# The first values of a fused attention and ELU kernel: from GpSimd's DMA queue to SyncE's, and into the buffer that first holds keys

## The chip, the cores and the metric

The kernel runs on one core of a Trainium2 chip. The metric is the device time of one execution in microseconds. Before the change it is 358.51 us, the median of three runs (358.48 to 359.07).

Engines are named as in the profile: PE (TensorE), DVE (VectorE), ACT (ScalarE), POOL (GpSimd) and SP (SyncE). PEld is PE's loading of weights. A q behind a name (SPq, POOLq) means an instruction that starts a DMA from that engine's instruction stream. Each engine takes its instructions strictly in the order written into its own stream; between engines they wait on semaphores.

## The reference

Eight batches with eight heads, 576 rows in each and a head size of 64, in float32:

```
proj = x @ w_phi                                   # 64 -> 128, for q and for k
proj = proj - max(abs(proj), axis=-1)
phi  = [exp(proj), exp(-proj)]                     # 256 features
kv   = phi(k)^T @ v ;  z = sum of phi(k) over the rows
out  = (phi(q) @ kv) / (phi(q) . z + 1e-6)         # linear attention
x    = out laid side by side over the heads        # 4608 x 512
h    = x @ w_in ;  g = elu(h) ;  y = g @ w_out     # 512 -> 2048 -> 512
```

The result is y, 4608 x 512 in float32.

## The kernel before, in words

**Tiling.** A batch is worked on in two "quads" of four heads each. Of the 576 rows of a head, 512 are the main part (four rows to each of 128 partitions) and 64 are the tail. A quad transposes its keys and queries on PE (L628), projects them (L689 keys and queries for the maxima, L864 queries again with features in the partitions), takes the maxima on DVE (L710), the exponentials on ACT (L757 keys, L944 queries), and the factors em that carry the maxima of the keys (L786, ACT). POOL multiplies the values by these factors: `scales` (L800), four products of the main part for a quad (`v_scaled`, L808, two for each half of the heads) and two of the tails (`v_tail_scaled`, L818). PE then sums keys times values (L992), and queries times that (L1060 and L1074). DVE combines and inverts (L1095, L1101, L1155), POOL makes x (L1172 in batch 0), and PE transposes x (L1259). From then on x @ w_in (L1354 for the first chunk, L1339 after), ELU and g @ w_out (L1443) run beside the attention of later batches.

**Order of the work.** A planner (`Planner.run`, L169) goes through the operations in simulated time and takes, on every engine, the free one of lowest rank; the ranks stand in a string (RANKS). Its result is the order in which instructions are written, and with it the order of every engine's stream. It also writes "fill" matmuls of zeros (L1651) where it expects PE to idle in the first 60 us. Semaphores follow from the tiles that an instruction reads and writes.

**Buffers.** `staged(b, n)` (L417) gives the tile for keys (n = 0), queries (1), values (2) and tails (3) of batch b, two buffers for each kind in turn. The values' buffers are float32, and the profile names both v_b. In the first stage a values' buffer is used for something else as well: the first four heads of keys of batch 0 are loaded into it as float32, two heads by ACT's queue and two by SP's (L1517), and ACT turns them into bf16 (`cast`, L1550). The tile is called k_first, and it is the buffer of the values of batch 1.

**Loads of the first batch.** `load_first` (L1578) writes them into POOL's stream, in the order of ranks: tails of k, heads 4 to 7 of k, heads 0 to 3 of v, heads 0 to 3 and 4 to 7 of q, heads 4 to 7 of v, tails of q. Then come keys and values of batch 1, and weights. A load of v of one half is 512 KB in float32. The tails of v go through SP's queue in eight DMAs (L456), the first four held back by a copy on DVE (`hold_tails`, L1637) until a maximum of the keys is there. v of batches 2 and later goes through SP's queue as well (L427).

**POOL's DMA semaphores.** POOL's DMAs take turns on eight semaphores, so the ninth DMA in its stream waits for the first to have landed, the tenth for the second, and so on. These waits stand in POOL's stream in front of the instruction, and everything behind waits with it.

Of the kernel before, what the change touches and what calls it, by code (L numbers as in the profile page):

```python
# [326 lines left out]
def kernel(  # L327
# [10 lines left out]
    nc = tc.nc  # L338
# [78 lines left out]
    def staged(b, n):  # L417
        if (b, n) not in kqv:
            kqv[b, n] = stage.tile(
                [P, 2 * H * D if n == 3 else BW],  # L420
                FP32 if n == 2 else BF16,
                name="kqvt"[n] + "_b",
            )
        return kqv[b, n]

    def load_main(eng, n, b, h0, h1):
        eng.dma_start(  # L427
            out=staged(b, n)[:, h0 * HW:h1 * HW].rearrange("p (h n) -> p h n", n=HW),
            in_=(k, q, v)[n][b, h0:h1, 0:MAIN, :].rearrange(
                "h (p t) d -> p h (t d)", t=NT  # L430
            ),
        )
# [34 lines left out]
    def load(name, mb, cost, fn, deps=()):  # L467

        key = -6.0 + 0.001 * len(landed)
        landed[name] = add(  # L470
            {"POOL": cost}, fn, deps or [landed["begun"]], key=key, load=mb,
            alone=3.0 + mb / plan.MB_PER_US_OF_ONE,
        )
# [1034 lines left out]
        tc.manual_schedule(engines={E.PE, E.DVE, E.Activation, E.Pool, E.SP})  # L1508
    )
    wst = moesm.tile([P, CHUNK], FP32, name="e_sb")[:, 0:F]  # L1510
    staged(0, 2)
    k_first = staged(1, 2)
    for c, eng in enumerate((nc.scalar, nc.sync)):
        w = wst[c * D:(c + 1) * D, :]
        if c:
# [56 lines left out]
    def load_kq_tails(n, b):  # L1572
        if n < 2:
            load((b, n, 1), 0.15, 0.7, lambda e: load_tails(nc.gpsimd, n, b))
        else:
            load_v((b, n, 1), 0.5, 2.6, lambda e: load_tails(nc.sync, n, b), [])

    def load_first(n, part):  # L1578
        if part == 1:
            load_kq_tails(n, 0)  # L1580
            return
        h = 2 * part
        load(
            (0, n, part), 0.57 if n == 2 else 0.54, 0.8,
            lambda e: load_main(nc.gpsimd, n, 0, h, h + 4),
        )

    for n, part in ((0, 1), (0, 2), (1, 0), (1, 1), (2, 0), (2, 1), (1, 2), (2, 2)):
        load_first(n, part)
# [98 lines left out]
```

## Time and profile before

| | |
|---|---|
| median of three runs | 358.51 us |
| the profiled execution's own time | 358.15 us |
| its span in the profile | 356.40 us |
| PE busy | 344.2 us (97%) |
| DVE, ACT, POOL busy | 264.4, 261.6, 243.5 us |
| clock granted to PE | 0.999 |
| DMA moved | 43.46 MB, mean 122 GB/s |

The profile gives times from the start of the span. A page of it shows totals over 356 us; the stage that the change touches is the first 45 us, and it is read from the timeline of single instructions, from the answers on who waited for whom, and from the DMA queues in short windows. In the DMA view, q0 (software_dynamic) is POOL's queue and q1 (hardware_dynamic) is SP's; q10 is ACT's. Behind each name stand packets, MB, and the time of the packets as a share of the 16 DMA engines, which goes over 100% where packets overlap. Sizes of a DMA are those of its destination. The fill matmuls count as busy PE, so a busy PE in the first 40 us isn't a PE with work.

### The profile page before, as it was taken

What the parts mean: (1) busy time and instruction counts of PE and PEld (TensorE: products, weight loads), DVE (VectorE), ACT (ScalarE), POOL (GpSimd) and SP (SyncE); (2) the same over time, 40 slices, a digit from 0 to 9 for tenths busy, and PEclk for the clock granted to TensorE, in tenths of its full rate; (3) what the DMA queues carried; (4) which work ended last, traced back from release to release, by engine and by line L of the source; (5) the groups of instructions that cost most, each with busy time, mean ns of one, the idle gap of its engine ahead of it and who ended that gap; (6) DMA issues with size and microseconds to landing.
All of it is one profiled execution on the core that took longest, in us unless ns stands there. A gap on an engine that the chain in (4) does not pass through costs nothing.

```text
span 356.4 us, 9086 instructions
## 1 busy us (share of the span) xinstructions
PE 344.2 (97%) x3439; PEld 205.5 (58%) x3484; DVE 264.4 (74%) x571; ACT 261.6 (73%) x575; POOL 243.5 (68%) x342
## 2 busy tenths in 40 slices
PE   7899999999999999999999999999999999999995
PEld 6677779556654664565655565555656545454444
DVE  6999799989997899878879867985888744425300
ACT  5998988997779888788878788868677545445311
POOL 8899987979867896988736983599365844335200
PEclk9999999999999999999999999999999999999999
DMA  7999999995896896799847422622032110010023
GB/s 164 256 234 209 206 194 217 180 179 162 129 140 131 139 228 106 161 181 138 96 92 204 96 65 64 195 64 65 32 93 64 30 36 29 29 62 29 29 62 87
DMA packets 84268, 43.46 MB, mean 122 GB/s; under 512 B 54656, under 2 KB 77696, under 8 KB 84224
## 3 DMA queue, kind: packets, MB, share of 16 engines
q1 hardware_dynamic: 57632, 26.59, 32.6%
q0 software_dynamic: 25760, 15.47, 30.6%
q10 hardware_dynamic: 832, 0.82, 0.8%
q8 instruction: 27, 0.44, 0.5%
q14 instruction: 17, 0.14, 0.1%
HBM read 36.77 MB, written 9.44 MB: 130 GB/s over the span
## 4 chain that ended last, share of the span: by engine, by line
PE 85%; ACT 6%; DVE 3%; DMA 3%; issue 2%; POOL 1%; ACTq 0%; POOLq 0%
PE po L1443 32%; PE ph L1339 31%; PE pkv L992 5%; PE pk L689 4%; PE ph L1354 4%; PE pn L1046 3%; DMA t_b<-in_q_dram 3%; PE pq L864 2%; ACT Eq L944 2%; ACT EK L757 2%; DVE tot L1095 1%; PE pnt L1074 1%; DVE tot L1101 1%; ACT e_sb L1367 1%; PE pk L671 1%
## 5 line engine op out<-in xcount | busy, mean ns | idle before, releaser
L1443 PE MATMUL po<-w_out_sb,gT 128*128 128x512 bf16 (+2 forms) x584 | 133.0, 368 | 1.3 <-issue 0.2
L1371 POOL TENSOR_SCALAR u_sb<-e_sb 128x512 bf16<-128x512 f32 x144 | 88.5, 620 | 66.6 <-ACT e_sb L1367 62.8
L1383 DVE SCALAR_TENSOR_TENSOR gT<-u_sb,ph 128x512 bf16<-128x512 bf16 x144 | 96.1, 679 | 36.0 <-POOL u_sb L1371 35.7
L1367 ACT ACTIVATE e_sb<-ph 128x512 f32<-128x512 f32 x144 | 86.5, 613 | 38.2 <-PE ph L1339 31.5
L1339 PE MATMUL ph<-xT,w_in 128*128 128x512 bf16 x427 | 106.0, 380 | 1.8 <-DVE gT L1383 0.5
L1443 PEld LDWEIGHTS <-gT 128*128 128x128 bf16 x608 | 55.2, 98 | 58.3 <-issue 2.5
L1339 PEld LDWEIGHTS <-w_in 128*128 128x128 bf16 x512 | 54.5, 114 | 45.6 <-issue 3.0
L757 ACT ACTIVATE EK<-pk 128x512 bf16<-128x512 f32 x128 | 68.4, 630 | 7.5 <-PE pk L689 6.7
L944 ACT ACTIVATE Eq<-pq 128x512 bf16<-128x512 f32 x128 | 68.7, 638 | 5.6 <-PE pq L864 5.5
L808 POOL TENSOR_TENSOR vs<-v_b,em 128x512 bf16<-128x512 f32 x64 | 65.9, 1048 | 0.1
L710 DVE TENSOR_REDUCE m_q<-pk 128x4 f32<-128x512 f32 (+1 forms) x80 | 48.2, 629 | 10.5 <-PE pk L689 8.5
L710 DVE TENSOR_REDUCE m_k<-pk 128x4 f32<-128x512 f32 (+1 forms) x80 | 47.6, 626 | 4.7 <-PE pk L689 4.6
L1143 POOL TENSOR_TENSOR x<-tot,rec 128x576 bf16<-128x576 f32 x28 | 31.8, 1157 | 10.2 <-DVE rec L1139 10.0
L1471 ACT COPY o_sb<-po 128x512 f32<-128x512 f32 (+2 forms) x29 | 16.3, 561 | 30.6 <-PE po L1443 28.7
L1095 DVE TENSOR_TENSOR tot<-pn,w 128x260 f32<-128x260 f32 x64 | 26.6, 423 | 8.6 <-PE pn L1046 7.2
L1101 DVE TENSOR_TENSOR tot<-tot,pn 128x260 f32<-128x260 f32 x64 | 26.4, 419 | 0.5
L1046 PEld LDWEIGHTS <-Eq 128*128 128x128 bf16 x448 | 20.1, 97 | 9.1
L818 POOL TENSOR_TENSOR vst<-v_tail,em 128x260 bf16<-128x260 f32 x32 | 19.7, 624 | 7.2 <-ACT em L786 7.2
L1046 PE MATMUL pn<-kv,Eq 128*128 128x65 bf16 x448 | 21.9, 193 | 0.1
L992 PE MATMUL pkv<-vs,EK 128*128 128x65 bf16 x512 | 20.5, 194 | 0.0
L992 PEld LDWEIGHTS <-EK 128*128 128x128 bf16 x512 | 18.4, 98 | 2.9 <-DVE m_q L710 0.4
L1354 PE MATMUL ph<-xT,w_in 128*128 128x256 bf16 x128 | 17.6, 274 | 0.2 <-DVE xT L1266 0.2
(93 smaller groups left out, 315.3 us busy)
## 6 DMA issues: line engine op xcount, KB each, us to landing
out_dram<-o_sb SPq DMA_DIRECT2D x32, 256.0 KB, 2.4
v_b<-in_v_dram SPq DMA_DIRECT2D x6, 1024.0 KB, 5.6
k_b<-in_k_dram POOLq DMA_DIRECT2D x7, 512.0 KB, 8.0
q_b<-in_q_dram POOLq DMA_DIRECT2D x7, 512.0 KB, 8.7
w_out_sb<-in_moe_w_out_dram POOLq DMA_DIRECT2D x4, 512.0 KB, 17.5
w_in<-in_moe_w_in_dram POOLq DMA_DIRECT2D x2, 1024.0 KB, 18.8
v_b<-in_v_dram POOLq DMA_DIRECT2D x2, 512.0 KB, 8.6
v_b<-in_v_dram POOLq DMA_DIRECT2D x1, 1024.0 KB, 13.8
```

The source lines that it names most:

```text
L710: nc.vector.tensor_reduce(dst, src, axis=AX.X, op=ALU.max, apply_absolute_value=True)
L757: nc.scalar.activation(EK()[:, 2 * c + par, sg, :] if c < 2 else EKt[:, sg, :], bank.tile[:, 0:n, :].rearrange("p a b -> p (a b)"), ACT.Ex ...
L808: nc.gpsimd.tensor_tensor(st["vs"][:, sg, :, r, 0:D], kqv[b, 2][:, o:o + 2 * HW].rearrange("p (c n d) -> p c n d", c=2, d=D), by_head(st[" ...
L944: nc.scalar.activation(dst, src, ACT.Exp, scale=1.0 - 2.0 * sg)
L992: nc.tensor.matmul(pkv[:, c, sg, :], st["EK"][:, 2 * s + t % 2, sg, (2 * c + t // 2) * F:(2 * c + t // 2 + 1) * F,] if t < NT else EKt[:, ...
L1046: nc.tensor.matmul(pt[:, t, :], st["Eq"][:, par, s, sg, o:o + P], st["kv"][:, s, c, sg, :], start=True, stop=True,)
L1339: nc.tensor.matmul(ph, w_in_of(ct, jt), xTs[ch][:, ct, :] if ch < B else xT_tail[:, ct // 2, :, ct % 2, :], start=(ct == 0), stop=(ct == N ...
L1354: nc.tensor.matmul(bank.tile[:, j, :], w_in_of(ct, jt + j), xTs[ch][:, ct, hf * CHUNK // 2:(hf + 1) * CHUNK // 2], start=(j == 0 and ct == 0),
L1367: nc.scalar.activation(t["e"], flat(bank.tile), ACT.Exp)
L1371: nc.gpsimd.tensor_scalar(t["u"], t["e"], -1.0, 1.0, op0=ALU.add, op1=ALU.mult)
L1383: nc.vector.scalar_tensor_tensor(dst, u, 0.0, bank.tile, op0=ALU.min, op1=ALU.max)
L1443: nc.tensor.matmul(bank.tile, gTs[ch][:, jt, tt * P:(tt + 1) * P], w_out_sb[:, jt, o0:o1], start=(jt == 0), stop=(jt == N_JT - 1),)
```

## The change

k_first becomes the buffer of the values of batch 0, where it was that of batch 1. The two halves of v of batch 0 leave POOL's stream and go to SP's, both at the place of the second one's operation. What the planner counts for these two operations, and all ranks, stay as they are.

```diff
-    staged(0, 2)
-    k_first = staged(1, 2)
+    k_first = staged(0, 2)
+    staged(1, 2)
...
         h = 2 * part
-        load(
-            (0, n, part), 0.57 if n == 2 else 0.54, 0.8,
-            lambda e: load_main(nc.gpsimd, n, 0, h, h + 4),
-        )
+
+        def heads(e):
+            if n < 2:
+                load_main(nc.gpsimd, n, 0, h, h + 4)
+            elif part:
+                for g in (0, 4):
+                    load_main(nc.sync, n, 0, g, g + 4)
+
+        load((0, n, part), 0.57 if n == 2 else 0.54, 0.8, heads)
```

In the streams of the engines this gives the following. POOL's has two DMAs fewer, and all else in it stands in the same order. SP's has the two DMAs right behind its load of k_first, ahead of the eight tails of v; the first of them waits for both of ACT's casts, since it writes over what they read. The load of v of batch 1 on POOL, which waited for the casts before, doesn't any more. PE, DVE and ACT have the same instructions in the same order.

The waits in POOL's stream shift with the two DMAs gone. The first load of w_out waits for no DMA (before: heads 4 to 7 of k); the tails of k of batch 1 wait for the tails of k of batch 0 (before: heads 0 to 3 of v); the first load of w_in waits for heads 4 to 7 of k (before: heads 0 to 3 of q). From the second load of w_out on, each DMA waits for the same one as before.

## Prediction

> **What bounds the kernel now.** The page gives PE 97% of the span, and the waits of PE between 44 and 300 us sum to 0.7 us, so from there on PE is full and a shift of the start is a shift of the end. The start is another stage. Busy time by stretches (us, then PE, PEld, DVE, ACT, POOL) shows it:
>
> ```profile
> 10.00:15.00 5.00, 4.07 (x71) 3.21 (x68) 4.68 (x10) 5.00 (x15) 4.20 (x7) 1.00 1.33 244
> 15.00:20.00 5.00, 4.44 (x73) 3.12 (x71) 4.80 (x10) 4.90 (x15) 4.99 (x8) 1.00 1.19 304
> 20.00:25.00 5.00, 4.92 (x99) 3.55 (x98) 4.48 (x12) 5.00 (x18) 4.98 (x9) 1.00 1.16 205
> 25.00:30.00 5.00, 4.50 (x109) 3.82 (x105) 4.89 (x17) 4.89 (x14) 4.98 (x8) 1.00 1.25 205
> 30.00:35.00 5.00, 4.71 (x76) 3.85 (x74) 4.96 (x17) 3.89 (x11) 4.96 (x8) 1.00 1.18 212
> ```
>
> POOL, DVE and ACT are all nearly full, and the DMA column is over 1. So I read POOL's timeline (start, duration, what; in brackets the idle time before and its releaser):
>
> ```profile
> 6.64 0.93 POOL L427 DMA_DIRECT2D k_b<-in_k_dram  x1
> 7.51 0.95 POOL L427 DMA_DIRECT2D v_b<-in_v_dram  x1
> 9.50 0.56 POOL L404 DMA_DIRECT2D w_out_sb<-in_moe_w_out_dram  x1 [1.04 <-DMA k_b<-in_k_dram]
> 10.84 0.60 POOL L436 DMA_DIRECT2D t_b<-in_k_dram  x1 [0.78 <-DMA v_b<-in_v_dram]
> 11.44 0.34 POOL L800 CAST vs<-em 128x32 bf16<-128x32 f32 x1
> 11.62 1.05 POOL L808 TENSOR_TENSOR vs<-v_b,em 128x512 bf16<-128x512 f32 x1
> ```
>
> From 10.84 us to about 45 us POOL has no gap that is listed; the two of 1.04 and 0.78 us are its only waits between 10 and 46. PE hangs on that stream directly; PE's longest wait of 10 to 46 us, in sum, is
>
> ```profile
> PE tr L1259 <- POOL x L1172: 0.5, 2, 0.3
> ```
>
> (29.59 and 30.74 us), and the vst products that end at 20.60 stand just ahead of the first sum of keys times values at 20.85. POOL from its first L808 on is therefore the line on which a delay passes to PE. ACT and DVE are as full, so a POOL that starts earlier gains little.
>
> **The DMA side.** POOL's queue works as a FIFO. v heads 0 to 3 are issued at 3.09 and land after 7.5 us (about 10.6, which releases POOL at 10.84); queries of batch 1, issued at 15.45, land after 16.7 us, at 32.15, and PE's L628 on them starts at 32.68. On SP's queue I look at how long an issue takes to its first packets while POOL's queue is busy. The first tail of v is issued at 8.47. The windows 8.4:9 and 12.5:13 have (packets, MB, share):
>
> ```profile
> q0 software_dynamic: 145, 0.12, 112.6%
> ...
> q0 software_dynamic: 165, 0.10, 108.8%
> q1 hardware_dynamic: 52, 0.01, 19.2%
> ```
>
> From 9 to 12.4 us there is no packet of q1: 4.0 us from issue to first packet. The transpose issued at 48.74 has its first packets at 52.7, again 4.0. With POOL's queue empty, at 84.0 us, v of a later batch has its first packets after about 1.6 us, runs at 347 to 369 packets of 1 KB per us, and lands 5.4 us after its issue.
>
> **What the Trainium skill says.** "DMA: Bandwidth & Descriptors", Issuing engines are not separate DMA queues: all queues run on the same 16 engines, and another issuer saves only its own issue time. The trace agrees: q0 falls from 382 packets per us alone to 243 beside q1's 238 (53:54 us). The same page, Queues, rings and completion order: engines go round robin over the queues by packet. That is this 1:1; beside the tails of v it was less for q1 (163 to 298 at 15:16). The same page, Latency and other measured facts: about 600 ns to a hardware queue's first byte. The trace shows 1.6 us free and 4.0 us under load; I use these.
>
> **The change part by part.**
>
> *Two issues leave POOL.* 0.77 + 0.79 = 1.56 us before its first product. POOL isn't late there, it waits afterwards. With the waits of the semaphores shifted, w_out's and t_b's issues are over at about 8.1, and L800 can start when em is there: the two L786 end at 10.53. So L808 could start at about 10.9 instead of 11.62, at best 0.7 us sooner, if its values are there.
>
> *SP's two issues.* The first waits for both casts; ACT's second ends at 5.54 + 0.62 = 6.16, so the first issue is at about 6.3. Behind it in SP's stream stand the second half and the tails of v. SP's tails before are held to 8.47 by DVE, and the two issues cost some 0.6 us each (0.59 and 0.57 for the two first ones on SP), so SP is free at 7.5: the issues cost nothing on SP itself; their packets are the matter.
>
> *When do heads 0 to 3 land?* First packet: 1.6 us later if free, 4.0 under load; POOL's queue is over 100% from 5.5 us on, hence I take 4.0, so 10.3. Then 512 packets of 1 KB. Without v in front of them, q and its tails are through POOL's queue by then, and the keys of batch 1 are in it, which are cast. Cast packets alone ran at 356 to 375 per us; shared 1:1 that is about 182 for each, so 512 packets take 2.8 us (bounds 1.4 alone, 3.9 at the tails' share of 163 to 298). Landing after the last packet 0.5 us (0.7 at 84.0; 0.2 to 0.4 for k_first). Sum 6.3 + 4.0 + 2.8 + 0.5 = 13.6. L808 starts at 13.6 instead of 11.62: **+2.0 us** on POOL's stream.
>
> *What the stall delays.* Behind L808 stand w_in's first load, three more products, q of batch 1, w_in, w_out, the tails' products. All the DMAs queue behind some 10 us of backlog in a FIFO, so they don't land later by being issued 2 us later. The products do come later: vst ends at 22.6, L992 starts at 22.8, x at 30.7 becomes 32.6, and PE with it. q of batch 1, at 32.15, no longer matters. PE's gaps before 37 us, including the fill of 0.50 at 36.23, come behind the same x, so they shift too, and I take 0 as absorbed. Cover for other delays: heads 4 to 7 of v are needed at 21.28 + 2.0 and should land near 18; the tails of v behind them in SP's queue land near 21, needed at 19.38 + 2.0. This is close.
>
> *Gains.* q and its tails land 2 to 4 us sooner. PE waited 0.4 us for the tails (15.54) and 0.17 for q, but ACT is full between 10 and 20 us (9.90 of 10), so this gives at most 0.1 us, and the later POOL stall hides it. Bytes are the same, so the backlog's end stays.
>
> Sum on the profiled execution: 358.15 + 2.0 = 360.15. The median of the runs is 0.36 higher: 358.51 + 2.0 = **360.5 us**.
>
> **Rivals.**
>
> *Quick start.* If SP's packets come after 1.6 us, as at 84.0, and share 1:1, v lands at 6.3 + 1.6 + 2.8 + 0.5 = 11.2, L808 starts about 0.4 us sooner, and with v at full rate (1.4 us) em is the limit, 0.7 sooner. PE then runs into q of batch 1 at 32.15, 0.5 us ahead of its L628: so -0.4 us, at most -0.7: 357.8 to 358.1. It decides from a landing before 11.6 on. For it: POOL's backlog is only 2 us old at 6.3. Against: 4.0 us in both loaded cases. Only its end, at -0.7, could be told from no change.
>
> *Hidden.* A landing at 11.6 to 12.3 (first packet after 2.5 to 3 us) gives 0 to +0.7: 358.5 to 359.2. PE's fills and ACT's backlog at 20 to 24 us could absorb a further few tenths.
>
> *SP's queue starved.* When POOL's queue reaches v of batch 1, its packets are large: 95 per us at 18:19, 3.7 KB each. At 1:1, SP's 1 KB packets get under 100 per us: heads 4 to 7 take 4 us and more, to about 18, the 512 tail packets behind them 3 to 5 us more, to 21 to 24. The third L818, at 20.70 + 2.0, then waits 1.3 us more; or, at the tails' share, heads 0 to 3 land at 14.7. Total +3.1 to +3.5: 361.6 to 362.0; both, +4.5: 363.0. Against: SP's 265 to 303 packets per us at 59:62 beside 97 to 183 of POOL's.
>
> **How the numbers follow.** Landing at 12.4 to 14.3, +0.8 to +2.7: 0.53. Starved: 0.22. Hidden: 0.17. Quick: 0.08, of which half passes 0.7. What can be told from no change is 0.2%, 0.7 us. Slower 0.75, same 0.21, faster 0.04. The range reaches from the hidden and quick cases near no change (358.3) to most of the starved (363.0); the likeliest case alone is 359.3 to 361.2.
>
> **What would show it.** Right: POOL's first L808 after a wait for the DMA of v of over 2 us, starting at 13 to 14.3; no POOL wait at L436; no q1 packets from 6.3 to about 10; q0's packets halving after; L602 of the tails of q without a wait; L1259 near 32.6; PE's busy stretch from 45 us on unchanged but for the shift. Wrong: first q1 packets of v before 8.5 us, or L808 before 12.3, or L1259 following DVE or ACT instead of POOL.

## The result, and the profile after

| | before | after |
|---|---|---|
| median of four runs each | 358.61 us (358.48 to 359.07) | 363.92 us (362.24 to 365.63) |
| the profiled execution's own time | 358.15 us | 362.24 us |
| its span | 356.40 us | 360.5 us |
| clock granted to PE | 0.999 | 0.993 |

The ratio is 1.0146 (95% interval 1.0097 to 1.0196). The kernel is 5.3 us slower by the medians and 4.1 us by the profiled executions. The forecast was 360.5 us with a range up to 363.0, so the direction was right and the time lies 0.9 us above the range. The runs after spread over 3.4 us, those before over 0.6.

POOL's timeline of the kernel after (start, duration, what; in brackets the idle time before and its releaser):

```profile
6.89 0.61 POOL L404 DMA_DIRECT2D w_out_sb<-in_moe_w_out_dram  x1
7.44 0.67 POOL L436 DMA_DIRECT2D t_b<-in_k_dram  x1
10.48 0.33 POOL L800 CAST vs<-em 128x32 bf16<-128x32 f32 x1 [2.38 <-ACT em L786]
15.65 1.05 POOL L808 TENSOR_TENSOR vs<-v_b,em 128x512 bf16<-128x512 f32 x1 [4.84 <-DMA v_b<-in_v_dram]
...
24.98 0.62 POOL L818 TENSOR_TENSOR vst<-v_tail,em 128x260 bf16<-128x260 f32 x1
```

The two waits of POOL's issues are gone, so that L800 starts when the factors are there, at 10.48; before, it stood behind the issue of t_b until 11.44, with the factors there at 10.53. Then POOL stands still for 4.84 us in front of its first product. L808 starts at 15.65 instead of 11.62, 4.03 us later, and the third tail product at 24.98 instead of 20.70.

The stretches of the first stage after (us, then PE, PEld, DVE, ACT, POOL; PE's clock, DMA share, GB/s):

```profile
10.00:15.00 5.00, 3.67 (x67) 3.01 (x66) 4.67 (x10) 5.00 (x14) 0.33 (x1) 1.00 1.25 246
...
20.00:25.00 5.00, 2.44 (x40) 1.72 (x39) 1.50 (x5) 3.25 (x11) 4.86 (x9) 0.94 1.16 208
25.00:30.00 5.00, 4.91 (x94) 4.08 (x93) 4.16 (x12) 2.90 (x8) 4.97 (x7) 0.72 1.21 202
```

POOL falls from 4.20 to 0.33 us of work between 10 and 15. The hole reaches PE one stage later: from 20 to 25 PE works 2.44 us instead of 4.92 and DVE 1.50 instead of 4.48. In the next row PE's clock is down to 0.72, which no row of before shows.

The answer on who waited for whom, from 0 to 46 us after (total, times, longest), names the same chain:

```profile
POOL vs L808 <- DMA v_b<-in_v_dram: 4.8, 1, 4.8
...
PE pkv L992 <- POOL vs L808: 1.6, 1, 1.6
```

and PE's timeline after shows where it arrives:

```profile
22.86 0.65 PE L992 MATMUL pkv<-vs,EK 128*128 128x65 bf16 x16 [1.62 <-POOL vs L808]
...
25.43 1.06 PE L992 MATMUL pkv<-vs,EK 128*128 128x65 bf16 x16
...
35.01 0.40 PE L1259 MATMUL tr<-ident,x 128*128 128x128 bf16 x4 [0.28 <-POOL x L1172]
```

In PE's timeline before, the first L992 and the same L1259 are at:

```profile
20.85 0.66 PE L992 MATMUL pkv<-vs,EK 128*128 128x65 bf16 x16
...
30.74 0.40 PE L1259 MATMUL tr<-ident,x 128*128 128x128 bf16 x4 [0.17 <-POOL x L1172]
```

The first L992 is only 2.0 us later, but its group then stands behind POOL's tail products. L1259 is 4.27 us later, the first L1354 is at 37.54 where it was at 33.37 (4.17 later), and the span is 4.1 longer. What POOL loses at L808, the end loses, one for one. The group at 25.43 has 16 matmuls of the same shape as the one at 22.86 and takes 1.06 us instead of 0.65: the clock was down to half from 24.4 to 27.8.

On SP's side, its timeline after has the two issues at 6.08 and the tails behind them:

```profile
6.08 2.02 SPq L427 DMA_DIRECT2D v_b<-in_v_dram  x2
8.37 12.96 SPq L456 DMA_DIRECT2D v_tail<-in_v_dram  x8
```

And the DMA queues after, in windows of one microsecond (packets, MB, share of 16 engines): the first row is 9:10, then come q1 (SP's queue) of 10:11 and 11:12, both queues of 12:13, q1 of 13:14, and both queues of 18:19:

```profile
q1 hardware_dynamic: 2, 0.00, 0.7%
...
q1 hardware_dynamic: 94, 0.10, 37.7%
...
q1 hardware_dynamic: 167, 0.17, 61.2%
...
q1 hardware_dynamic: 174, 0.18, 63.8%
q0 software_dynamic: 174, 0.08, 60.6%
...
q1 hardware_dynamic: 168, 0.16, 58.9%
...
q0 software_dynamic: 83, 0.30, 90.3%
q1 hardware_dynamic: 85, 0.03, 13.2%
```

The first packets come just before 10.0, 3.9 us after the issue. The two queues then share the engines packet by packet, 174 and 174. Counted up, 2 + 94 + 167 + 174 = 437 packets of SP's have gone by 13.0, and at 168 per us the 512th goes at 13.45. The prediction had the last packet of the first half at 13.1. Yet L808 starts at 15.65.

What lies between the count and the product can be read from the single increments of the semaphore that POOL waits for, one from each of the 16 DMA engines as its part has landed (us; worked out from the trace's semaphore events):

```
first half of v, after:  13.16 13.42 13.48 13.55 13.58 13.67 13.69 13.72
                         13.76 13.78 13.99 14.00 14.13 14.21 14.92 15.51
heads 0 to 3 of v, before: first 8.06, middle 8.72, last 10.56
```

The middle engine landed at 13.7. The last one landed 1.8 us after it, and L808 starts 0.14 us after that one. Was the last engine late with its packets, or with what comes after them? Some 0.3 to 0.5 us ahead of each of the sixteen increments, SP's queue has a packet of 4 bytes; the first of these goes at 12.79 and the last at 15.04. So the engines weren't done together: the first was through with its part at 12.8, the last only at 15.0. Those done went on with the second half of v, and the 512 packets of the count aren't all of the first half. The sum failed in the time that the packets take. From the last engine's closing packet to its increment it was 0.47 us, close to the predicted 0.5. The packets of the first half can be counted alone in `first_half` below. "DMA: Bandwidth & Descriptors" of the Trainium skill, section Why a DMA increments its semaphore by 16 and not by 1, says that the engines finish independently and that only the full count means that all data has landed. The trace agrees: fourteen of sixteen increments by 14.21 released nothing.

### The profile page after: what moved, and what is told of

The parts are those of the page before. It is cut to its first block, busy times and chain, and to the rows that moved or that the text cites. A ratio compares the mean times of both kernels' runs of the same rounds, so it can differ in the third digit from the quotient of the medians.

```text
span 360.5 us, 9130 instructions
## 1 busy us (share of the span) xinstructions
PE 347.9 (97%) x3484; PEld 206.7 (57%) x3484; DVE 264.9 (73%) x571; ACT 261.8 (73%) x575; POOL 241.8 (67%) x340
## 4 chain that ended last, share of the span: by engine, by line
PE 89%; DMA 4%; POOL 3%; DVE 1%; ACT 1%; issue 1%; ACTq 0%; SPq 0%; DVEq 0%; POOLq 0%
PE po L1443 35%; PE ph L1339 31%; PE pkv L992 5%; PE ph L1354 4%; PE pk L689 4%; PE pn L1046 4%; DMA v_b<-in_v_dram 3%; PE pq L864 2%; POOL vs L808 1%; DMA v_b<-in_k_dram 1%; PE pnt L1074 1%; PE pk L671 1%; PE tr L628 1%; ACT EK L757 1%; DVE tot L1095 0%
## 5 line engine op out<-in xcount | busy, mean ns | idle before, releaser
L1443 PE MATMUL po<-w_out_sb,gT 128*128 128x512 bf16 (+2 forms) x608 | 136.4, 368 | 0.0
L1339 PE MATMUL ph<-xT,w_in 128*128 128x512 bf16 x448 | 107.6, 380 | 0.7 <-DVE gT L1383 0.5
L808 POOL TENSOR_TENSOR vs<-v_b,em 128x512 bf16<-128x512 f32 x64 | 65.9, 1048 | 4.9 <-DMA v_b<-in_v_dram 4.8
L1143 POOL TENSOR_TENSOR x<-tot,rec 128x576 bf16<-128x576 f32 x28 | 31.7, 1154 | 10.5 <-DVE rec L1139 10.2
L992 PE MATMUL pkv<-vs,EK 128*128 128x65 bf16 x512 | 20.9, 195 | 1.6 <-POOL vs L808 1.6
L992 PEld LDWEIGHTS <-EK 128*128 128x128 bf16 x512 | 18.9, 99 | 4.6 <-issue 1.8
L1354 PE MATMUL ph<-xT,w_in 128*128 128x256 bf16 x128 | 17.6, 274 | 0.2 <-DVE xT L1266 0.2
```

The costliest lines, as they stand in the source:

```text
L808: nc.gpsimd.tensor_tensor(st["vs"][:, sg, :, r, 0:D], kqv[b, 2][:, o:o + 2 * HW].rearrange("p (c n d) -> p c n d", c=2, d=D), by_head(st[" ...
L992: nc.tensor.matmul(pkv[:, c, sg, :], st["EK"][:, 2 * s + t % 2, sg, (2 * c + t // 2) * F:(2 * c + t // 2 + 1) * F,] if t < NT else EKt[:, ...
L1339: nc.tensor.matmul(ph, w_in_of(ct, jt), xTs[ch][:, ct, :] if ch < B else xT_tail[:, ct // 2, :, ct % 2, :], start=(ct == 0), stop=(ct == N ...
L1354: nc.tensor.matmul(bank.tile[:, j, :], w_in_of(ct, jt + j), xTs[ch][:, ct, hf * CHUNK // 2:(hf + 1) * CHUNK // 2], start=(j == 0 and ct == 0),
L1443: nc.tensor.matmul(bank.tile, gTs[ch][:, jt, tt * P:(tt + 1) * P], w_out_sb[:, jt, o0:o1], start=(jt == 0), stop=(jt == N_JT - 1),)
```

## The experiments

Each edit is made to the kernel after, save one that says otherwise, and the line numbers of some shift by up to three. In the expectations, A is the prediction's mechanism (the first half of v lands late, and POOL's wait passes to the end one for one), A2 that POOL's packets set the pace of SP's on each engine, B a loss by PE's lower clock after its idle time, D a second half of v that delays the last engines of the first, E the tails of v landing late behind the second half, F a cost of SP's queue against POOL's, G a landing of the first half that itself varies from run to run, and H packets of SP that come fast once POOL's queue has run dry.

All runs in one table. "Second half" is the start of POOL's first product of heads 4 to 7, which is at 21.28 before, so it counts what POOL lost up to there; growth of the span is against 356.40. "Against before" is the ratio of the times to those of the kernel before that were measured with them, and is not formed from the two medians.

| run | median, us | against before (95%) | first L808 | second half | span's growth |
|---|---|---|---|---|---|
| the change (result) | 363.92 | 1.0146 (1.0097 to 1.0196) | 15.65 | 25.57 | 4.1 |
| `again` | 364.36 | 1.0159 (1.0130 to 1.0188) | 16.01 | 25.65 | 4.5 |
| `again2` | 364.54 | 1.0173 (1.0153 to 1.0192) | 15.75 | 26.85 | 5.3 |
| `fills` | 365.25 | 1.0180 (1.0146 to 1.0213) | 16.00 | 28.02 | 8.3 |
| `no_hold` | 360.01 | 1.0038 (1.0021 to 1.0056) | 10.23 | 20.54 | 1.1 |
| `first_half` | 362.16 | 1.0100 (1.0073 to 1.0127) | 15.73 | 25.34 | 4.2 |
| `first_half_fills` | 362.35 | 1.0114 (1.0100 to 1.0127) | 15.37 | 24.99 | 3.5 |
| `second_last` | 363.58 | 1.0153 (1.0139 to 1.0167) | 15.64 | 25.50 | 5.1 |
| `pool_held` | 359.94 | 1.0058 (1.0038 to 1.0078) | 13.54 | 23.16 | 1.7 |
| `behind_tails` | 369.46 | 1.0311 (1.0297 to 1.0325) | 22.44 | 32.05 | 11.5 |
| `no_tails` | 362.06 | 1.0117 (1.0090 to 1.0145) | 13.86 | 23.49 | 1.7 |
| `second_half` | 362.61 | 1.0124 (1.0099 to 1.0149) | 11.71 | 26.63 | 6.7 |
| `quiet` | 362.24 (one run) | none | 13.61 | 25.56 | 4.1 |

**The change once more.** No edit.

> The changed kernel once more, unaltered. Theory A (the wait of POOL for the values passes one to one to the end): whatever time the first L808 starts at in the profile, minus 11.62 us, is the growth of the span over 356.4 us, within 0.4 us; in the first profile it started at 15.65 and the span grew by 4.1. Theory B (part of the loss is TensorE's clock, which was granted at 0.94 and 0.72 between 20 and 30 us after PE's idle time): the growth is larger than the shift of L808, by up to 1.5 us, in executions with a lower mean clock. Median 362.5 to 365.

The median is 364.36 us, and in the profile POOL waits 5.28 us and the first L808 comes 4.39 us later for a span 4.5 us longer. So A holds inside a profiled execution. The median is 1.7 us above the profile's own 362.69: something varies between executions, and adds.

**Filling PE's idle time.** The idea was to keep PE's clock up with matmuls of zeros.

```diff
             def kv(e, s=s, bank=bank):
+                if i == 0 and s == 0:
+                    plan.fill(bank.index, 30)
                 pkv = psum(bank, [P, 2, 2, D1], FP32, "pkv")
```

> The changed kernel with 30 more fill matmuls of zeros on PE ahead of the first sum of keys times values (L992), where PE sat idle for 1.62 us. Nothing else is altered, and the fills end before the products of POOL are there (21.2 + 30 x 0.056 = 22.9 us, L992 ran from 22.86). Theory A (only POOL's wait counts): the median stays that of the unaltered one within 0.5 us. Theory B (the clock counts): the granted clock stays at 1.00 from 20 to 30 us, and the median comes down by 0.7 us or more, towards 362.3, with less spread.

The fills came ahead of the second group of L992, from 26.3 us on, when the clock was down already, and so ran at half of it. The run tells nothing for or against B. It showed something else; POOL's timeline of this kernel:

```profile
24.28 1.20 POOL L818 TENSOR_TENSOR vst<-v_tail,em 128x260 bf16<-128x260 f32 x2 [0.56 <-DMA v_tail<-in_v_dram]
...
27.44 0.62 POOL L818 TENSOR_TENSOR vst<-v_tail,em 128x260 bf16<-128x260 f32 x1 [1.68 <-DMA v_tail<-in_v_dram]
```

POOL waits a second time, 2.2 us in all, for the tails of v. In the first two profiles these had landed about when they were needed (24.85 for a product at 24.98).

**Without the hold.** k_first goes back to batch 1's buffer, so that nothing holds v of batch 0, which SP issues at 2.0 us.

```diff
-    k_first = staged(0, 2)
-    staged(1, 2)
+    staged(0, 2)
+    k_first = staged(1, 2)
```

> The values on SP's queue as in the change, but the first keys stay in the buffer of batch 1's values as before, so SP doesn't wait for the casts and issues at about 2.0 us instead of 6.1. Theory A (the hold makes the values late): packets of the values before POOL's queue is full, landing before 9 us, first L808 at about 10.8, when em is there; 0.3 to 0.8 us faster than before, 357.8 to 358.3. Rival (SP's queue itself loses to POOL's queue, hold or not): landing after 11.6, L808 later than 12, and slower than before by 0.5 us or more.

The median is 360.01 us, 1.8 above that of before (358.21), where a gain of 0.3 to 0.8 was expected: a miss. POOL was served as expected, PE was not. POOL's timeline of this kernel:

```profile
10.23 1.04 POOL L808 TENSOR_TENSOR vs<-v_b,em 128x512 bf16<-128x512 f32 x1
```

and PE's timeline of it:

```profile
10.11 0.62 PE L628 MATMUL tr<-ident,k_b 128*128 128x128 bf16 x8 [1.43 <-DMA k_b<-in_k_dram]
...
12.99 1.06 PE L628 MATMUL tr<-ident,q_b 128*128 128x128 bf16 x8
```

L808 starts 1.39 us earlier than before, but heads 4 to 7 of the keys come later: PE transposes them at 10.11 instead of 9.27, and the queries behind them at 12.99 instead of 11.82, at a low clock after the wait (1.06 us instead of 0.62). POOL's lead ends in a wait of 2.0 us for DVE at L1172. Early values take packets from the keys, which are needed first.

**Only the first half on SP's queue.** Heads 4 to 7 go back to POOL's queue.

```diff
-                for g in (0, 4):
-                    load_main(nc.sync, n, 0, g, g + 4)
+                load_main(nc.sync, n, 0, 0, 4)
+                load_main(nc.gpsimd, n, 0, 4, 8)
```

> Only heads 0 to 3 of v go through SP's queue behind the casts; heads 4 to 7 stay on POOL's queue at their old place, between the queries and the tails of the queries. In the change, fifteen of the sixteen engines had landed the first half by 14.92 and the last at 15.51, while half of them were done by 13.72. Theory D (the second half behind it on SP's ring holds up the last engines): all land by 14.2, L808 at 14 or before, 360.5 to 361.5. Theory A2 (POOL's queue, packet by packet, sets the pace on each engine): the last engine again 1.5 us or more behind the middle one, L808 at 14.8 to 16, 361.8 to 364.

POOL's timeline of this kernel:

```profile
15.73 1.05 POOL L808 TENSOR_TENSOR vs<-v_b,em 128x512 bf16<-128x512 f32 x1 [4.92 <-DMA v_b<-in_v_dram]
```

L808 is as late as with both halves: middle engine 14.3, last engine 15.58. So the second half isn't what delays the last engine of the first, and D falls; the numbers are those that A2 asked for. Here the packets of the first half can be told from all others of SP's queue by their size in the trace (1 KB; those of the tails have 256 bytes). The first goes at 10.02, the 256th at 12.46, the 480th at 13.84 and the 512th at 15.21, which is 5.2 us after the first, and the last increment comes 0.37 us later. In `first_half_fills` and `second_last` the same 512 take 4.9 and 4.6 us, and the last increment comes 0.5 and 0.8 us later. The median is 362.16, the four runs lie within 0.36 us of each other, and the median agrees with the profile (362.37). The tails landed at 16.2 to 18.0. Against `again`, measured with it, leaving the second half on POOL's queue saves 364.36 - 362.16 = 2.2 us, and nearly all of the spread.

**The second half behind the tails.**

```diff
+            def tails(e):
+                load_tails(nc.sync, n, b)
+                if b == 0:
+                    load_main(nc.sync, n, 0, 4, 8)
...
-                for g in (0, 4):
-                    load_main(nc.sync, n, 0, g, g + 4)
+                load_main(nc.sync, n, 0, 0, 4)
```

> Both halves of v on SP's queue behind the casts, as in the change, but the second half behind the four tails of v instead of ahead of them. In the two profiles of the change, the last of the tails landed at 24.85 and 24.93 us, just before L818 took them at 24.98 and 25.07; in the profile of the run with fills, L818 waited 2.2 us for them. Theory E (in executions without a profile the tails behind the 512 packets of the second half come later than POOL needs them, and this is what the change loses beyond the 4.1 us of its profile): tails landed by 18 us, span as in the profile of the change or 0.3 us less, median 361.8 to 362.6 with a spread under 1 us. Theory B (the rest is TensorE's clock after PE's idle time): median 363.5 to 364.5 and spread of 2 us or more, as for the change.

Three of the four tails were there by 17.1 and the last at 18.7, and the spread fell to 1.0 us, near what E asked. But the median, 363.58, is in B's range, so neither holds as it stands. Heads 4 to 7 now landed at 25.43, and POOL waited 0.21 us for them: small tails ahead of them, POOL's large packets beside them. POOL's second half starts 4.22 us late and the span grows by 5.1. The stretch of this kernel that stands for the rest:

```profile
25.00:30.00 5.00, 4.94 (x70) 3.95 (x69) 3.98 (x11) 2.33 (x7) 4.64 (x6) 0.50 1.21 201
```

PE is full there at half its clock, for 6.8 us in all; that goes with the 0.9 us by which the span grew more than POOL lost.

**The first half on SP, with fills in the idle time.** As `first_half`, and the 30 fills with `s == 1`, which puts them ahead of the first L992.

> As the run with only the first half on SP's queue (362.16 us, which is 3.9 over before), with 30 fill matmuls ahead of the first L992, where PE is idle from 21.2 to 22.9. The fills of the earlier run had gone in ahead of the second L992, behind the idle time, and ran at half clock. Theory B (the clock costs): no window of half clock at 25 to 30 us, and 0.3 us or more faster than 362.16. Theory A (POOL's wait alone): the window may go, the median stays at 361.9 to 362.4.

The same stretch of this kernel:

```profile
25.00:30.00 5.00, 4.14 (x91) 3.14 (x90) 4.93 (x17) 3.96 (x10) 4.97 (x8) 1.00 1.21 204
```

In this profile the clock stays at full all the way; of the other three executions, two have a mean clock below 1 (0.994 and 0.998). The median doesn't move (362.35; `first_half` 362.16). Set against what POOL lost, the span of this profile grew 0.2 us less (3.5 for 3.71), and that of `first_half` 0.1 us more (4.2 for 4.06). From these two single profiles I estimate about 0.3 us for one stretch of low clock. B may add that much, and it is not what made the change cost 4 us.

**The same hold, on POOL's queue.** Both halves stay in batch 0's held buffer, issued by POOL behind the tails of q.

```diff
...
+                load_tails(nc.gpsimd, n, b)
+                if n and b == 0:
+                    for g in (0, 4):
+                        load_main(nc.gpsimd, 2, 0, g, g + 4)
...
-            elif part:
-                for g in (0, 4):
-                    load_main(nc.sync, n, 0, g, g + 4)
```

> The buffer as in the change and the casts' hold as well, but both halves of v go through POOL's own queue, behind the tails of the queries and ahead of the keys of batch 1: same hold, other queue. Theory F (the queue: on POOL's queue the values stand in line behind at most 4 us of data, ahead of everything that comes after, and share with nobody): landing of the first half at about 12.5 (issue at 6.2, q and its tails through by 9.3, 1.8 us of packets, 2.2 us from the last packet to landing at the slowest engine), L808 at 12.6, 1.0 us slower than before, 359.0 to 359.6; keys of batch 1 land where they did before. Rival (the hold itself is what costs, whatever the queue): L808 at 15 or later, 362 or more.

POOL's timeline of this kernel:

```profile
13.54 1.04 POOL L808 TENSOR_TENSOR vs<-v_b,em 128x512 bf16<-128x512 f32 x1 [2.26 <-DMA v_b<-in_v_dram]
```

L808 comes 1.92 us later than before, where 1.0 was expected, and the span grows by 1.7. F was right in direction: of the 4 us that a held first half costs on SP's queue, the hold with the later place in the order makes some 1.9 (POOL also waits 1.2 us for the casts in front of the issue), and SP's queue the rest.

**Both halves behind the tails on SP.** The prediction's mechanism at more than twice its size. The edit is as in `second_last`, with both halves moved.

> The change with both halves of v behind the four tails on SP's queue, which are held to 8.4 us, so that the first half is issued at about 11 instead of 6.1. Theory A (POOL's wait passes one to one to the end): L808 later than 15.65 by some 3 to 5 us, at 18.5 to 20.7, and the span longer than that of the change by the same, within 0.4 us; 365.5 to 367.5. If ACT, DVE or the loads of weights take over as the limit, the span would grow by clearly less than L808's start.

POOL's timeline of this kernel:

```profile
22.44 1.04 POOL L808 TENSOR_TENSOR vs<-v_b,em 128x512 bf16<-128x512 f32 x1 [12.22 <-DMA v_b<-in_v_dram]
```

L808 was expected at 18.5 to 20.7 and came at 22.44, 6.8 us after that of the unaltered change, and the span is 7.4 us longer than there. One for one holds at this size too, and the other 0.6 us go with a clock of 0.981 instead of 0.993. Again it was the landing that I put too early, not the passing on.

**The change a third time**, to see the tails late in it.

> The changed kernel once more, for the chip that it shares with the three others of this call. Median 363.5 to 364.6, spread 2 us or more, and a growth of the span in the profile of L808's shift plus 0 to 0.3 us if TensorE has one window of half clock (3.4 us), and plus about 1 us if it has two.

POOL's timeline of this kernel:

```profile
23.97 1.20 POOL L818 TENSOR_TENSOR vst<-v_tail,em 128x260 bf16<-128x260 f32 x2 [0.50 <-DMA v_tail<-in_v_dram]
...
26.27 0.62 POOL L818 TENSOR_TENSOR vst<-v_tail,em 128x260 bf16<-128x260 f32 x1 [0.83 <-DMA v_tail<-in_v_dram]
```

This is the unaltered kernel, with the second wait in it: 0.50 + 0.83 = 1.3 us. With the 4.13 us of L808, POOL is 5.57 us late at the second half, and the span grew by 5.3, as much as the medians of the result differ by. The last two tails landed at 24.52 and 26.13.

**Without those tails.** The four loads of batch 0's v tails are left out.

```diff
-            load_v((b, n, 1), 0.5, 2.6, lambda e: load_tails(nc.sync, n, b), [])
+            load_v((b, n, 1), 0.5, 2.6, lambda e: b and load_tails(nc.sync, n, b), [])
```

> The change without the four loads of v's tails of batch 0 (the tails of that batch's values stay zero, so its sums leave them out); all computation on them stays, only nothing waits for them. Theory E (in the change the tails, behind the second half on SP's ring, land later than POOL needs them in executions without a profile, where they make most of the spread and of the 1.5 us between the profile and the median): median at the profile's 362.2 to 362.7 or below, spread under 1.2 us. Theory G (the landing of the first half itself and the clock's windows make the spread): median within 0.6 us of the unaltered change, spread of 2 us or more.

The median falls to 362.06, 2.5 below `again2`, as E asked. The spread doesn't fall as E asked: 359.90 to 364.45. The profile is the fastest of the six, with L808 at 13.86, since the casts ended 0.7 us sooner and the last engine was only 0.8 us behind the middle one. Without tails that can be late, the time still goes over 4.5 us, so something else varies too. The first half's landing does between profiles (13.71 here, 15.51 to 15.87 in the three of the unaltered change), but of the other five executions there is no trace. E and G each hold in part, and this run doesn't divide the cost between them.

**The second half alone.** This one starts from the kernel before: only heads 4 to 7 go to SP's queue, behind the tails; heads 0 to 3 and k_first stay as they were.

```diff
+            def tails(e):
+                load_tails(nc.sync, n, b)
+                if b == 0:
+                    load_main(nc.sync, n, 0, 4, 8)
...
-            lambda e: load_main(nc.gpsimd, n, 0, h, h + 4),
...
+        def heads(e):
+            if n < 2 or not part:
+                load_main(nc.gpsimd, n, 0, h, h + 4)
...
```

> The kernel before with one part of the change: only heads 4 to 7 of v go to SP's queue, behind the four tails of v; heads 0 to 3 stay on POOL's queue at their place, and the first keys stay in the buffer of batch 1's values. With one DMA fewer in front, the load of t_b that held POOL until 10.84 waits for heads 4 to 7 of k (9.2 us) and no longer for heads 0 to 3 of v. Theory: L800 starts when em is there (10.5) and L808 when v is (10.8 to 11.2); the second half lands at 18 to 20, before 21.3. 0.2 to 0.7 us faster, 357.5 to 358.0. Rival (ACT and DVE are full in this stage and q of batch 1 lands at 32.15 as before): no change within 0.2 us. Other rival (the tails or the second half are late on SP's queue, as in the change): slower by 0.5 us or more.

POOL's timeline of this kernel:

```profile
26.63 2.06 POOL L808 TENSOR_TENSOR vs<-v_b,em 128x512 bf16<-128x512 f32 x2 [4.22 <-DMA v_b<-in_v_dram]
```

A gain was hoped for; it is 4.4 us slower (362.61). The load was issued at 12.07 and its last engine landed at 26.57, 14.5 us later for 512 KB. L800 didn't come sooner than before either (11.54): it waits for the factors, which came at 11.48 here and at 10.53 before, PE's L628 on the keys running at half clock (1.06 us instead of 0.62). The profile is of the slowest of the six executions (364.92), so its span grew more than the median.

**A quiet POOL queue.** POOL's first loads of batch 1's keys and values and of w_out are written behind the first L808, so that POOL's queue runs dry while the first half of v comes in.

```diff
+            while later:
+                later.pop(0)()
...
-        load(
-            (1, n, 0), 1.1 if n == 2 else 1.04, 0.93,
-            lambda e: load_main(nc.gpsimd, n, 1, 0, 8),
-        )
+        def main(e):
+            if n == 1:
+                load_main(nc.gpsimd, n, 1, 0, 8)
+            else:
+                later.append(lambda: load_main(nc.gpsimd, n, 1, 0, 8))
+
+        load((1, n, 0), 1.1 if n == 2 else 1.04, 0.93, main)
...
```

> The change with three of POOL's loads (keys and values of batch 1, first part of w_out) moved behind the first L808, so that POOL's queue runs dry at about 9.3 us, while heads 0 to 3 of v are on SP's queue. Its time says nothing on the change, since PE gets those keys late; the landing does. Theory H (the 4 us from SP's issue to its first packet are the time that POOL's queue needs for what it already holds, and from then on packets go one for one): first packets no later than in the change (9.9 us), 300 or more per us once POOL's queue is dry, and the first half landed by 12 us at all sixteen engines. Rival (SP's queue is slow here by itself): landing after 14 again.

The queues of this kernel at 12:13:

```profile
q1 hardware_dynamic: 370, 0.36, 104.7%
...
q0 software_dynamic: 13, 0.00, 3.1%
```

With POOL's queue dry, SP's goes at 370 packets per us instead of 174. That part of H holds. The first packets came at 9.55, 3.8 us after the issue at 5.77; POOL's queue was over 110% busy up to 10.0, so the run doesn't test what these 4 us are. The landing was 12.3 at the middle engine and 13.47 at the last, where 12 or less was expected for all. With POOL's queue nearly gone the last engine is still 1.2 us behind the middle one, so A2 can't be the whole reason. Even so, the load costs POOL 2 us (L808 at 13.61), and the three issues behind it then delay the second product to 17.75.

## Why the prediction was right or wrong

- **What bounds the stage: right.** POOL from its first L808 on passes its delay to PE and to the end. In the result 4.03 us became 4.1; in `behind_tails` 10.8 became 11.5; in `pool_held` 1.92 became 1.7. The rivals that hid the landing, or made it quick, fall with L808 at 15.65.
- **SP's issues cost nothing: right.** They end at 8.1, and the tails are issued at 8.37 (8.47 before). POOL's two issues saved were worth nothing, since L800 waits for the factors and L808 for v. Nor were the queries and their tails, which landed 1.1 to 2.2 us sooner (the prediction said 2 to 4).
- **First packet after 4.0 us: right,** 3.9, with no q1 packets until just before 10. Its reason, a loaded queue, fits the runs, though none tests it apart. In `no_hold`, issued at 2.00 with POOL's queue at 1% in 3:4, v's first packet came by 4.5 at the latest (the 257th of 1 KB on SP's queue; 256 are keys). In `quiet`, with POOL's queue still full, it came after 3.8 us.
- **Sharing one to one: right,** 174 to 174.
- **"512 packets take 2.8 us": wrong, and this is the step that failed.** The sum divides the load by what the queue moves as a whole, as if the sixteen engines were one pipe that is done at one time. The product waits for the last of them, and the first ones don't help it: in the change they go on with the second half. Counted alone, the packets of the first half take 4.6 to 5.2 us (`first_half`, `first_half_fills`, `second_last`), longer also than the prediction's upper bound of 3.9. Of this the first 480 make 3.5 to 4.0 and the last 32 another 0.9 to 1.4. In the result it is 5.1 us, from 9.96 to the last engine's closing packet at 15.04, so the term was 2.3 us too small.
- **"Landing after the last packet 0.5 us": right,** 0.47 in the result and 0.4 to 0.8 where it can be counted. The sum's 13.6 fits the landing of the middle engine (13.7), which releases nothing. The last one came at 15.2 to 15.9 in the seven profiles with this place of the load (the result, both repeats, `fills`, `first_half`, `first_half_fills`, `second_last`). The distance was to be had from the kernel before, in which heads 0 to 3 of v landed at 8.72 at the middle engine and at 10.56 at the last. With 1.8 us more the sum gives 15.4 for L808, and 362.3 for the median. The 1.6 us from there to 363.92 belong in part to the next point, and in part to differences between executions that stay open.
- **The tails: "near 21, needed at 19.38 + 2.0. This is close": the place was right, the handling wrong.** The last two tails landed at 24.15 and 24.85 in the result's profile and at 24.52 and 26.13 in `again2`. I gave the starved queue a chance of its own, 0.22, as if it excluded the likeliest case. They add: a first loss of some 4 us and, in some executions, a second wait (1.3 us in `again2`, 2.2 in `fills`). That is part of the median's 5.3 us and of its spread; how large a part stays open, since `no_tails` spreads as well.
- **"PE's gaps shift too": roughly right, with a term left out.** After its idle time PE was granted half the clock for a while, an estimated 0.3 us for one such stretch. For two there is no one price: against POOL's loss up to the second half, the span grew 0.3 us less in `again2`, and 0.9 to 1.6 us more in `second_last`, `second_half` and `fills`.
- **Open.** Which DMA engines are the slow ones, and why the sixteen aren't done together; what makes up SP's 4 us to the first packet; and how the differences between executions divide between the first half's landing and the tails. No variant that ran beat the kernel before; the nearest, `pool_held` and `no_hold`, cost 1.8 us.

## What to carry to other kernels

A wait for a DMA ends with the slowest of its sixteen engines, so take a landing time from the last increment of a comparable load under comparable traffic, not from the count of a queue's packets, which holds the next load's too, and not from a quiet stretch: here that was about 2 us of a loss of 4. When a load is moved to another queue, price what stands behind it in that queue as well, and add that price to the first loss instead of treating it as another case. And if a buffer's first tenant decides when a load may start, that start plus the queue's whole latency must still come before the first reader, which here left nothing: 6.1 + 3.9 us is 10.0 before a single packet, and the reader was ready at 10.8.

## What the runs showed of the hardware

- **The spread of the engines.** Of the first half on SP's queue at this place the last engine landed 1.1 to 2.0 us after the middle one (1.2 in `quiet`, 0.8 in `no_tails`); of heads 0 to 3 of v before, on POOL's queue, 1.8 us. At 84.0 us before, in a quiet stretch, it was 0.4 us for 1 MB.
- **Small packets beside large ones.** Sharing is by packet, not by byte: at 18:19 after, 83 packets of POOL's moved 0.30 MB and 85 of SP's 0.03 MB. The four tail loads of 32 KB issued at 8.4 to 10.5 took 13.8 to 14.4 us to land, where they took 6.1 to 6.7 before. This is what "DMA: Bandwidth & Descriptors" of the Trainium skill, Queues, rings and completion order, leads one to expect of a round robin by packet; its size was the surprise.
- **After a pause of PE its clock falls.** After PE's idle time the clock is at half for a stretch of 3.4 us (24.4 to 27.8 in the result's profile, two such stretches in `again2`). "TensorE: Matmul & The Clock Gate" of the Trainium skill, Part 1: The HAM clock gate, gives a free-running window of 3413 ns and half the rate after an idle one. The trace agrees in length (3.41 us). It also shows that PE need not stand still all the time: in the 3.41 us before the clock fell it was busy for 1.06. With 30 fills in the idle time the profile has the clock at full, and the median didn't move by anything that could be measured.
